# Block 3's x on one DMA queue, its scaling and its sums moved: a change to a linear attention and SwiGLU kernel

## The chip, the cores and the metric

The kernel runs on one core of a Trainium2 chip. A core has five engines, each with its own queue of instructions: TensorE (PE, matrix products; PEld is its loading of weights), VectorE (DVE), ScalarE (ACT), GpSimd (POOL) and SyncE (SP), which here only issues transfers. Transfers are issued from the queues of SP and ScalarE (in the profile SPq and ACTq) and carried out by 16 DMA engines. The metric is the time of one execution on the device in microseconds; less is better. The median of three runs before is 1026.51 us (1025.12 to 1028.15).

## The reference, cut to what matters

```python
def _attn_ref(q, k, v, g_norm):
    kv = np.einsum('bhsd,bhse->bhde', k, v)
    out = np.einsum('bhsd,bhde->bhse', q, kv)
    rms = np.sqrt(np.mean(out * out, axis=-1, keepdims=True) + 1e-06)
    return (out / rms * g_norm).astype(np.float32)

def _moe_ref(x, w_gate, w_val, w_out):
    g = x @ w_gate
    silu = g * (1.0 / (1.0 + np.exp(-g)))
    val = x @ w_val
    return (silu * val @ w_out).astype(np.float32)

# q, k, v: (8, 8, 576, 64), float32
x = np.ascontiguousarray(attn_out.transpose(0, 2, 1, 3)).reshape(4608, 512)
# w_gate, w_val: (512, 1536); w_out: (1536, 512)
return _moe_ref(x, w_gate, w_val, w_out)
```

A linear attention without a softmax, normalised and multiplied by a gain per channel, gives x; a SwiGLU feed-forward network with 1536 hidden channels follows.

## The kernel before, in words

The 4608 tokens are nine blocks of 512. Block 0 is computed with plain products. Blocks 1 and 2 are computed one at a time with a scheme of seven block products in place of eight (P1 to P7, on sums of sub-blocks of x and of the weights), and blocks 3 to 8 in pairs of blocks, with the scheme applied twice. Each block has an "up" part (gate, value, silu and their product, which gives h) and a "down" part (h times w_out). While one block is in its up part, the attention of a later block is computed in between.

The up part of a single block (class Up) runs over six pairs of hidden tiles. In `ahead`, pairs and steps are keyed as (pair, product), with pairs counted from 0; the sixth pair is 5. For each pair the products come in the order P1, P5, then P4 and P3 of the pair before, then P6, P2, P7; after the sixth pair follow its own P3 and P4 (`end`). Products go to banks of PSUM: b for P1, P6, P7, P4; a for P2; c for P5 and, accumulated onto it, P3. Each product has a follow-up on another engine:

- P1 and P6: ScalarE copies bank b (L677, L681).
- P2: VectorE adds bank a to a piece called s (L707, in the profile under the helper's line L130).
- P7: ScalarE copies bank b (L711) and applies silu to s (L714); VectorE adds bank c (L715, under L130). Behind it stand the "owed" sums of h of the pair before (L130 and L131, 128x256).
- P4: ScalarE applies silu (L724), POOL multiplies (L132).
- P3: VectorE adds bank c (under L130), POOL multiplies (L132).

During block 2's up part the x of block 3 is made. Its attention is normalised and turned by 32 x 32 squares on VectorE (L510); `place_x` then moves the squares to their places with 16 small DMAs within SBUF (L522), eight from SP's queue and eight from ScalarE's; `gain_x` multiplies by the gain, two activations on ScalarE (L529); `sum_steps` makes four sums of sub-blocks on VectorE (L539 to L542, under L130 and L131, arena<-arena 128x512). In the dictionary, `place_x` stands behind the fifth pair's P1, `gain_x` behind its P7, and the sums behind the sixth pair's P5. The sums go through a list of chores, of which at most two are taken after each product.

In block 2's up part VectorE's instructions keep the order in which the code makes them (`in_order`); on the other engines the framework's scheduler may move an instruction within what its data allow. In the built program the scaling of block 3's x stands on ScalarE between L711 and L714 of the sixth pair.

On SP's queue, around the placements, stand the loads of block 4's q (L333, 32 of them), then the placements, then 16 sends of weight pieces to DRAM (L920), then the loads of keys and values of block 5 (L312). Block 3's x lies in the first 14 units of a large SBUF tile, the arena, in the place of gate and value weights that have been sent away by then; the pieces sent at L920 lie from unit 16 up.

Of the kernel before, what the change touches and what calls it, by code (L numbers as in the profile page):

```python
# [18 lines left out]
def kernel(  # L19
# [41 lines left out]
    nc = tc.nc  # L61
# [65 lines left out]
    PAIRED = 3  # L127
# [102 lines left out]
    class Att:  # L230
# [284 lines left out]
        def place_x(self):  # L515
            src = self.turned.rearrange("p i (x c) -> p (i x) c", c=P)
            dst = self.x[:, 0:4].rearrange("p o k (t c) -> p (o k t) c", c=P)
            rows = [slice(32 * r, 32 * (r + 1)) for r in range(4)]
            for a in range(4):
                for b in range(4):  # L520
                    queue = nc.scalar if b % 2 else nc.sync
                    placed = queue.dma_start(out=dst[rows[b], :, rows[a]], in_=src[rows[a], :, rows[b]])  # L522
                    if b % 2 == 0:
                        self.placed = placed
# [421 lines left out]
    def raw_steps(j):  # L946


        for t, os in kept(j):
            yield lambda t=t, os=os: send_leaf(j, os, (1,), t[:, :, 0, 0])  # L950
            yield lambda t=t, os=os: send_leaf(j, os, (2, 3), t[:, :, 1].rearrange("p o e c -> p o (e c)"))

    def chunks(t):

        return t.rearrange("p f (s c) -> p (f s) c", c=P) if len(t.shape) == 3 else t.rearrange("p a b c -> p (a b) c")

    def kept_steps(j, room):


        for i, (t, os) in enumerate(kept(j)):  # L960
            b11, b12, b22 = t[:, :, 0, 0], t[:, :, 0, 1], t[:, :, 1, 1]
            to = room[:, 8 * i : 8 * (i + 1)].rearrange("p (o r) c -> p o r c", r=4)
            t2_ = to[:, :, 0]
            yield lambda b22=b22, b12=b12, t2_=t2_: sub(nc.vector, t2_, b22, b12)
            yield lambda b11=b11, t2_=t2_: add(nc.vector, t2_, t2_, b11)
            yield lambda t=t, t2_=t2_, to=to: sub(
                nc.vector, to[:, :, 2:4], t[:, :, 1], t2_.unsqueeze(2).to_broadcast([P, 2, 2, P])
            )
            yield lambda t2_=t2_, os=os: send_leaf(j, os, (6,), t2_)
            yield lambda b11=b11, t2_=t2_, to=to: sub(nc.vector, to[:, :, 1], b11, t2_)  # L970
            yield lambda to=to, os=os: send_leaf(
                j, os, (7, 4, 5), to[:, :, 1:4].rearrange("p o r c -> p o (r c)")
            )
        if j < 2:
            yield from raw_steps(j)
# [269 lines left out]
    def visit(ffn, att, gs, apart=False):  # L1245

        with tc.issue_after(ffn.multiplied.ins):
            for g in gs:
                att.kv(g, apart)
        if att.n < B:  # L1250
            ffn.visited = att.positions

    def ahead(ffn, att, then):

        def load(att, i):
            return lambda: ffn.sends.extend(att.quarter_steps(i, (0, 1), (nc.sync,)))

        def first():
            visit(ffn, att, (0, 1))
            ffn.sends += [load(att, 0), lambda: then.load_kv(0), load(att, 1)]  # L1260

        def turn(i):
            ffn.chores.append(lambda: att.turn_q(i))

        def second():
            visit(ffn, then, (0,), True)
            ffn.sends.append(lambda: then.load_kv(1))

        def half(i):
            with tc.issue_after(ffn.multiplied.ins):  # L1270
                att.heads(i, range(NS), (m_psum, m_psum))
            ffn.visited = att.multiplied
            ffn.chores += att.chores(i)
            if i:
                ffn.chores += att.turn_steps()

        def rest():
            for i in range(2):
                load(then, i)()

        def raw():
            for j in range(2, NP):
                ffn.sends += raw_steps(j)

        def sums():
            ffn.chores.extend(att.sum_steps())

        for j in (NP - 2, NP - 1):
            ffn.making.extend(kept_steps(j, chunks(h_alone[:, NF - 4 :]) if j == NP - 1 else chunks(xi_alone)))

        return {
            (0, 1): first, (1, 6): lambda: turn(0), (1, 7): second, (2, 1): lambda: half(0), (2, 6): lambda: turn(1),
            (2, 7): rest, (3, 1): lambda: half(1), (3, 7): lambda: visit(ffn, then, (1,), True), (4, 1): att.place_x,
            (4, 2): raw, (4, 7): att.gain_x, (5, 5): sums,
        }

    def alone(n):
# [27 lines left out]
        elif n == 1:  # L1325

            def third():
                visit(ffn, nxt, (0,))
                nxt.load_kv(1)

            def two_thirds():
                visit(ffn, nxt, (1,))
                for i in range(2):
                    nxt.load_q(i)

            ffn.up({(1, 7): third, (3, 7): two_thirds})
            nxt.turn()
            for g in range(2):
                blocks[PAIRED].load_kv(g)
        else:  # L1340
            with in_order(nc.vector.engine):
                ffn.up(ahead(ffn, nxt, blocks[PAIRED + 1]))
            nxt = blocks[PAIRED + 1]
            nxt.turn()
            for g in range(2):
                blocks[PAIRED + 2].load_kv(g)
# [82 lines left out]
```

## Time and profile before

| | us |
|---|---|
| median of three runs | 1026.51 |
| the profiled execution | 1027.35 |
| its span, first to last instruction | 1025.6 |
| PE busy | 998.6 |
| DVE busy | 667.0 |
| POOL busy | 368.6 |
| ACT busy | 232.1 |

Stages by time in the span, with the time in which PE was busy:

| stage | from, to | PE busy of |
|---|---|---|
| block 0 | 0 to 113.4 | 102.18 of 113.40 |
| block 0 down, block 1, its down | 113.4 to 265 | 149.60 of 151.60 |
| block 2 up | 265 to 363 | 89.85 of 98.00 |
| block 2 down | 363 to 401.5 | 38.50 of 38.50 |
| blocks 3 to 8 | 401.5 to 1025.6 | 618.51 of 624.10 |

The profile comes from one execution. A group of instructions is named by its line in the code, its engine, its operation and output<-input by the program's names; in the timeline a row gives start, duration, engine, line and how often, and in brackets the idle time of the engine just ahead with what ended it. That releaser is inferred; where an instruction waits for several things, it is the one that came last. SPq and ACTq rows are the issuing of transfers, not the transfers.

### The profile page before, as it was taken

Reading aid. Unit: us, or ns where it says so; the run is one execution under the profiler, and the core shown is the slowest. Engines: PE = TensorE matmul, PEld = TensorE weight load, DVE = VectorE, ACT = ScalarE, POOL = GpSimd, SP = SyncE. Lnnn points to the kernel's source line nnn. Section 1 sums busy time; section 2 is a strip of 40 time slices with the busy share of each in tenths; the row PEclk is TensorE's granted clock in tenths of the full one; section 3 lists DMA queues with packets and bytes.
Section 4 is the critical chain, followed back from the end, with each engine's and each line's share of the span. In section 5 each row is a group of like instructions: output and inputs, shape, how many; then the busy total and the mean of one; then the engine's idle time right before and its main releaser. Section 6 shows DMA issues by size and latency. Waiting matters only on the chain.

```text
span 1025.6 us, 17091 instructions
## 1 busy us (share of the span) xinstructions
PE 998.6 (97%) x6506; PEld 832.9 (81%) x6506; DVE 667.0 (65%) x1118; ACT 232.1 (23%) x367; POOL 368.6 (36%) x290
## 2 busy tenths in 40 slices
PE   5999999999999699999999999999999999999998
PEld 4544688888888588888888888888888888888887
DVE  2999797759766466566666846666767566666211
ACT  2765112221122211212111212112112121121100
POOL 0000273426343140454556003555650026546600
PEclk9999999999999899999999999999999999999999
DMA  8689643756663836676753265667321654553011
GB/s 233 201 255 263 119 90 118 226 161 148 179 163 63 214 67 156 168 212 166 169 139 58 89 149 160 156 173 182 101 32 52 144 156 144 153 145 97 1 42 42
DMA packets 254290, 143.23 MB, mean 140 GB/s; under 512 B 149504, under 2 KB 236544, under 8 KB 254208
## 3 DMA queue, kind: packets, MB, share of 16 engines
q1 hardware_dynamic: 219264, 137.67, 49.8%
q10 hardware_dynamic: 34880, 4.46, 2.7%
q8 instruction: 52, 0.85, 0.4%
q14 instruction: 30, 0.25, 0.1%
q0 software_dynamic: 64, 0.00, 0.0%
HBM read 104.99 MB, written 28.70 MB: 130 GB/s over the span
## 4 chain that ended last, share of the span: by engine, by line
PE 86%; DVE 5%; SPq 3%; DMA 2%; POOL 1%; ACT 1%; issue 1%; ACTq 0%; DVEq 0%; POOLq 0%
PE b L811 21%; PE b L661 21%; PE c L661 12%; PE c L811 11%; PE a L661 5%; PE a L811 5%; PE b L1154 4%; PE c L1154 4%; SPq L333 1%; DVE arena L131 1%; PE m L431 1%; PE m L370 1%; DMA arena<-in_v_dram 1%; POOL t L131 1%; DVE r L130 1%
## 5 line engine op out<-in xcount | busy, mean ns | idle before, releaser
L811 PE MATMUL b<-arena,t 128*128 128x256 f32 x1008 | 244.5, 381 | 0.0
L811 PEld LDWEIGHTS b<-arena,t 128*128 128x128 f32 x1008 | 190.0, 190 | 29.6 <-DVE r L130 2.5
L130 POOL TENSOR_TENSOR r<-r 128x256 f32<-128x256 f32 (+1 forms) x90 | 94.8, 1054 | 246.4 <-DMA t<-w 149.5
L130 DVE TENSOR_TENSOR r<-b,r 128x512 f32<-128x512 f32 (+1 forms) x234 | 138.9, 606 | 60.1 <-PE b L811 54.8
L130 DVE TENSOR_TENSOR r<-c,r 128x512 f32<-128x512 f32 (+1 forms) x170 | 104.6, 624 | 107.6 <-PE c L811 41.0
L132 POOL TENSOR_TENSOR arena<-r 128x1024 f32<-128x1024 f32 (+1 forms) x54 | 101.4, 1892 | 115.1 <-DVE r L130 89.0
L131 POOL TENSOR_TENSOR t<-wo 128x512 f32<-128x512 f32 x54 | 76.6, 1439 | 175.3 <-DVE wo L130 104.8
L130 DVE TENSOR_TENSOR r<-a,r 128x512 f32<-128x512 f32 x93 | 59.2, 636 | 108.6 <-PE a L661 71.0
L811 PE MATMUL c<-arena,t 128*128 128x256 f32 x504 | 122.5, 379 | 0.8 <-ACT r L825 0.8
L131 DVE TENSOR_TENSOR arena<-arena 128x512 f32<-128x512 f32 (+3 forms) x96 | 104.2, 1100 | 18.1 <-PE b L661 14.0
L811 PEld LDWEIGHTS c<-arena,t 128*128 128x128 f32 x504 | 95.6, 190 | 14.4 <-ACT r L825 1.2
L661 PE MATMUL b<-wo,arena 128*128 128x256 f32 x432 | 98.3, 382 | 0.6 <-issue 0.5
L661 PE MATMUL b<-t,arena 128*128 128x256 f32 x432 | 96.4, 379 | 1.4 <-POOL s L130 0.7
L661 PEld LDWEIGHTS b<-t,arena 128*128 128x128 f32 x432 | 81.9, 190 | 13.2 <-POOL s L130 1.1
L661 PEld LDWEIGHTS b<-wo,arena 128*128 128x128 f32 x432 | 81.2, 190 | 12.9 <-issue 0.9
L825 ACT COPY r<-b 128x512 f32<-128x512 f32 x54 | 31.6, 585 | 190.6 <-PE b L811 190.6
L131 POOL TENSOR_TENSOR t<-arena 128x512 f32<-128x512 f32 x36 | 51.1, 1432 | 59.5 <-PE c L661 20.2
L811 PE MATMUL a<-arena,t 128*128 128x256 f32 x252 | 66.1, 379 | 0.0
L811 PEld LDWEIGHTS a<-arena,t 128*128 128x128 f32 x252 | 47.9, 190 | 6.5
L661 PE MATMUL c<-wo,arena 128*128 128x256 f32 x216 | 48.2, 379 | 0.2 <-DVE r L130 0.2
L661 PE MATMUL c<-t,s 128*128 128x256 f32 x216 | 48.1, 379 | 0.0
L661 PE MATMUL a<-wo,arena 128*128 128x256 f32 x216 | 48.1, 379 | 0.0
(105 smaller groups left out, 1228.4 us busy)
## 6 DMA issues: line engine op xcount, KB each, us to landing
t<-w SPq DMA_DIRECT2D x180, 256.0 KB, 3.1
out_dram<-r SPq DMA_DIRECT2D x17, 512.0 KB, 2.9
ld<-in_k_dram SPq DMA_DIRECT2D x26, 288.0 KB, 4.6
ld<-in_v_dram SPq DMA_DIRECT2D x26, 288.0 KB, 5.8
t<-w SPq DMA_DIRECT2D x54, 128.0 KB, 2.2
ld<-in_moe_w_gate_dram SPq DMA_DIRECT2D x12, 512.0 KB, 4.7
ld<-in_moe_w_val_dram SPq DMA_DIRECT2D x12, 512.0 KB, 4.7
ld<-in_moe_w_out_dram SPq DMA_DIRECT2D x12, 512.0 KB, 4.9
```

Of the source, the lines that this page charges most:

```text
L130: add = lambda e, o, a, b: e.tensor_tensor(out=o, in0=a, in1=b, op=OP.add)
L131: sub = lambda e, o, a, b: e.tensor_tensor(out=o, in0=a, in1=b, op=OP.subtract)
L132: mul = lambda e, o, a, b: e.tensor_tensor(out=o, in0=a, in1=b, op=OP.mult)
L333: queue.dma_start(out=to[32 * r : 32 * (r + 1), j, g0:g1], in_=q[b, 4 * i + 2 * j + h, s0 : s0 + 32 * (g1 - g0), 32 * d : 32 * (d + 1)].re ...
L370: self.positions = nc.tensor.matmul(self.kv_ps[r][u * D : (u + 1) * D, g, :], lhsT=k[:, u, c, :], rhs=v[:, u, c, :], start=(c == 0), stop= ...
L431: self.multiplied = nc.tensor.matmul(self.ps[i][u][p : p + D, t, j, :], lhsT=self.qt[rows, tile_t, head, p : p + D], rhs=kvs[b % 3][rows, ...
L661: self.ffn.multiplied = nc.tensor.matmul(banks[e][:, e], lhsT=lhsT, rhs=rhs, start=first and i == 0 and (e == 0 or banks[0] is not banks[1 ...
L811: self.ffn.multiplied = nc.tensor.matmul(ps[:, i], lhsT=stream.use(self.ffn.n, self.j, o, p), rhs=self.operand(o, p), start=first and i == ...
L825: nc.scalar.copy(out=dst, in_=ps)
L1154: nc.tensor.matmul(t, lhsT=w[f // 2][:, i, P * (f % 2) : P * (f % 2 + 1)], rhs=x[:, i, of], start=(i == 0), stop=(i == NS - 1),)
```

## The change

In `place_x`, block 3 (`PAIRED` is 3) issues all 16 placements from SP's queue; for the other blocks half of them stay on ScalarE's. In `ahead`, the scaling moves from behind the fifth pair's P7 to behind the sixth pair's P5, and the sums from behind the sixth pair's P5 to behind its P6.

```diff
             for a in range(4):
                 for b in range(4):
-                    queue = nc.scalar if b % 2 else nc.sync
+                    queue = nc.scalar if b % 2 and self.n != PAIRED else nc.sync
                     placed = queue.dma_start(out=dst[rows[b], :, rows[a]], in_=src[rows[a], :, rows[b]])
                     if b % 2 == 0:
                         self.placed = placed
...
             (2, 7): rest, (3, 1): lambda: half(1), (3, 7): lambda: visit(ffn, then, (1,), True), (4, 1): att.place_x,
-            (4, 2): raw, (4, 7): att.gain_x, (5, 5): sums,
+            (4, 2): raw, (5, 5): att.gain_x, (5, 6): sums,
```

In the changed program's order of instructions, PE's and POOL's are the same as before. ScalarE has the scaling behind L714 of the sixth pair instead of ahead of it, and eight DMA issues fewer. SP has 16 placements in a row where it had eight. On VectorE the four sums stand behind the fifth pair's P3 addition and the sixth pair's P2 addition, the first two of them ahead of the sixth pair's P7 addition, the last two behind it and behind the owed sums of h.

## The prediction

> **What bounds the kernel now.** I read the page first, then PE's waits, the table of stages around the only place where its clock share drops, the timeline there, and SP's waits. The page:
>
> ```profile
> span 1025.6 us, 17091 instructions
> PE 998.6 (97%) x6506; PEld 832.9 (81%) x6506; DVE 667.0 (65%) x1118; ACT 232.1 (23%) x367; POOL 368.6 (36%) x290
> PEclk9999999999999899999999999999999999999999
> ```
>
> TensorE is the bound: 27 us of the span are not PE. One slice, the 14th, has a lower clock, and it lies where the change works. The longest wait in PE's list:
>
> ```profile
> PE c L661 <- DVE r L130: 8.9, 3, 8.2
> ```
>
> One wait of 8.2 us on an addition of VectorE. The stages around it (PE, PEld, DVE, ACT, POOL busy, granted clock, DMA share, GB/s):
>
> ```profile
> 348.00:356.60 8.60, 0.46 (x3) 0.06 (x1) 5.37 (x8) 3.28 (x4) 1.64 (x1) 0.75 1.01 274
> 356.60:360.00 3.40, 3.39 (x8) 2.77 (x9) 0.71 (x2) 0.02 (x1) 0.00 (x0) 0.50 1.06 228
> 360.00:363.00 3.00, 3.00 (x9) 2.42 (x9) 0.69 (x1) 0.00 (x0) 1.26 (x1) 0.58 0.96 203
> 363.00:366.00 3.00, 3.00 (x16) 2.64 (x15) 0.72 (x2) 0.60 (x1) 1.26 (x1) 1.00 0.01 1
> ```
>
> PE stands still from 348.46 to 356.61 and then runs at half clock until about 362.5. The timeline of the hole, instruction by instruction:
>
> ```profile
> 346.57 1.89 PE L661 MATMUL b<-arena,t 128*128 128x256 f32 x8
> 348.50 0.58 ACT L711 COPY r<-b 128x512 f32<-128x512 f32 x1 [2.87 <-PE b L661]
> 348.98 2.19 ACT L529 ACTIVATE arena<-arena,gain 128x1024 f32<-128x1024 f32 x2
> 351.20 0.69 DVE L130 TENSOR_TENSOR arena<-arena 128x512 f32<-128x512 f32 x1 [10.37 <-DMA w<-arena]
> 351.81 0.68 DVE L131 TENSOR_TENSOR arena<-arena 128x512 f32<-128x512 f32 x1
> 352.41 0.68 DVE L130 TENSOR_TENSOR r<-c,r 128x512 f32<-128x512 f32 x1
> 353.01 2.35 DVE L131 TENSOR_TENSOR arena<-arena 128x512 f32<-128x512 f32 x2
> 355.28 0.68 DVE L130 TENSOR_TENSOR r<-a,r 128x512 f32<-128x512 f32 x1
> 355.88 0.68 DVE L130 TENSOR_TENSOR r<-c,r 128x512 f32<-128x512 f32 x1
> 355.99 0.63 ACT L714 ACTIVATE r<-r 128x512 f32<-128x512 f32 x1 [4.83 <-DVE r L130]
> 356.61 3.78 PE L661 MATMUL c<-arena 128*128 128x256 f32 x8 [8.15 <-DVE r L130]
> ```
>
> This is read backwards. PE's P3 of the sixth pair accumulates onto bank c, which the sixth pair's P7 addition (L715, the row at 355.88) must have read; it ends at 356.56 and PE starts 0.05 later. Ahead of it in VectorE's queue stand the first sum of block 3's x (351.20) and five others. That sum had held VectorE for 10.37 us. The view names a DMA w<-arena as its releaser; I don't believe it: the sum reads x, which the scaling L529 writes, and the second scaling ended at 348.98 + 2.19 = 351.17, 0.03 before it; the weight pieces sent at L920 lie in the arena from unit 16 up, block 3's x in units 0 to 14. The scaling in turn waited for nothing but its place in ScalarE's queue, behind L711 (348.50): the last of its placing DMAs was issued at 341.04. On the issuing side, the waits of SP's queue and then the timeline:
>
> ```profile
> SPq L333 <- DMA arena<-r: 11.3, 1, 11.3
> ```
>
> ```profile
> 326.94 5.83 ACTq L522 DMA_DIRECT2D arena<-r  x6
> 335.67 5.37 SPq L522 DMA_DIRECT2D arena<-r  x8
> 341.08 9.55 SPq L920 DMA_DIRECT2D w<-arena  x16
> ```
>
> SP's loads of q (L333) waited 11.3 us for a placing DMA that ScalarE had yet to issue, because in the built program the DMAs of the two queues take their completion counters in turn from the same eight, and a DMA waits for the last one on its counter; SP's own eight placements therefore start only at 335.67.
>
> **What the Trainium skill says.** "TensorE: Matmul & The Clock Gate", section "What's actually happening": the array falls to half clock after an idle window of about 3.4 us and recovers after a busy one, the windows running freely. The trace agrees: clock share 0.75, 0.50, 0.58, 1.00 in the four rows above. The same page, "Architectural detail", says that ScalarE and VectorE are strict first-in-first-out; the ten microseconds in which VectorE has a ready addition of bank c behind a waiting sum show it. "DMA: Bandwidth & Descriptors", "Issuing engines are not separate DMA queues": both issuers' DMAs run on the same 16 DMA engines, and a second issuer saves only its time to initiate. Here initiating costs 5.37/8 = 0.67 us each on SP, so eight more cost 5.4 us of SP. "ScalarE: Activation LUTs", "What ACT_TABLE_LOAD costs", prices a switch of sets at 2.66 us, which a silu directly ahead of a scaling might bring; the trace has two such loads in all (1283 ns each, the last at 31.4), with copies, scalings and silus mixed ever since, so I take none.
>
> **The change, part by part.** *Placement on SP alone.* ScalarE loses eight issues. They delayed the fifth pair's P4 silu (L724) to 332.81, 3.3 us after its product, but PE ran through, so this is worth 0. SP gains eight issues and loses the 11.3 us wait: 15 loads of q are left at 316.2 (the first of the 16 in SP's row from 315.80 to 335.50 is issued then), about 0.5 each as on their unhindered stretches, done near 324; placement can start when the transposes end (322.48 + 2.36 = 324.84). Sixteen at 0.67 + 0.04 last 11, to 336, and land 2.3 to 4.3 later (all L522 DMAs): by 340. Were the old start of 335.67 kept, the last would be issued by 346.6 and landed by 349 to 351. Queued behind on SP: 16 weight pieces (9.6 us) and the key and value loads of block 5. In before they started at 341.08 and 350.73; now about 336 and 346 (at worst 346.6 and 356). SP next waits 21.5 us for PE, so both ends of this cost 0.
>
> *Sums one product on.* On VectorE the changed program's order is: fifth pair's P3 addition, sixth pair's P2 addition, two sums, sixth pair's P7 addition, the fifth pair's two h sums, then the other two sums. So the P3 addition runs at 343.3 (PE's product of 341.39 + 1.89) and the P2 addition at 344.84 + 1.89 = 346.73, done by 347.5: both leave the hole. Of the sums two instead of four stand ahead of the P7 addition.
>
> *Scaling behind P5.* On ScalarE the scalings now stand behind the sixth pair's silu L714 instead of ahead of it. That silu waited for the P2 addition (355.99 before); that is now done at 347.5, so it starts right behind L711 at 348.98. From there (starts of successive ScalarE instructions lie about 0.10 less than a duration apart):
>
> silu 348.98 to scaling 349.51 (0.63 - 0.10); scalings end 349.51 + 2.19 = 351.70; first sum 351.73, second 352.34, P7 addition 352.94, ended 353.62; PE at 353.67.
>
> Before, PE started at 356.61: **2.94 us less**. Cross-check: out of VectorE's stretch go the P3 addition (352.41 to 353.01), two sums (353.01 to 355.28) and the P2 addition (355.28 to 355.88), 3.47 in all; the silu ahead of the scaling gives 0.53 back. If the silu cost a table load, 2.66 would return; if nothing, 0; I take 0.
>
> *Clock.* The hole shrinks from 8.15 to 5.21 us. Half clock lasted from 356.61 to about 362.5, worth half of 5.9, 2.95 us. Is 5.2 us idle enough to drop the clock again? Windows fall anywhere; in the worst position the hole is split into 2.6 and 2.6. At the program's end the clock record falls to half at 1024.7 with the last matmul ended at 1022.2, a window with 2.5 idle: so a split hole drops it too. I take the loss as unchanged: in both kernels half clock then lasts one to two windows, 3.4 to 6.8 us by the page's figure, an estimate of 1.7 to 3.4 lost. Bounds of what a shorter hole can bring: 0 and 2.95.
>
> *Behind it.* From 363 to 401.5 PE is busy for all of 38.5 us, and from there 618.5 of 624.1; what precedes (h sums, POOL's products) hangs on PE's P3 and P4 and moves with them. A shift at 356 should reach the end whole.
>
> Sum: -2.94. The profiled execution took 1027.35 around its span of 1025.6, 0.84 above the median of 1026.51; so 1024.4 for it and **1023.6** for the median.
>
> **Rivals.** *The clock stays up:* the hole is too short. For it: 5.2 is not two windows. Against: the fall at the end after 2.5 idle. Time: 1026.51 - 2.94 - 2.95 = 1020.6. *Given back:* a transfer ordered by SP or POOL ends a later stage, so the shift is absorbed. For it: the DMA share is 1.0 in the hole. Against: PE's wait list shows no DMA after the start. Time: 1026.5. *Slower, placement late on one queue:* if SP's q loads still end at 335.67 and an issue takes 1.2 (the slowest L522 issue) rather than 0.67, the sixteenth ends at 354.9, lands at 359.2 with 4.3, and the scaling starts 9.7 later than I say: PE at 363.4, time 1026.5 + 6.8 = 1033.3. It decides once the last landing passes 349.5, and the kernel is slower once it passes 352.45. Against: the load ahead of it no longer waits for ScalarE.
>
> **How the numbers follow.** No change means within 0.3%, 3.1 us, about what can be told here; my forecast lies just inside it, so its own spread splits it. Forecast 0.84 (own range 1022 to 1025.3; 0.40 beyond 0.3%, 0.43 within, 0.01 slower), clock stays up 0.08 (faster), given back 0.05 (same), placement late 0.03 (slower). Faster 0.48, same 0.48, slower 0.04. The three times shown spread over 3 us, partly where the clock's windows fall. Range 1020.3 to 1025.8: it takes in the clock rival and leaves out the other two.
>
> **What would show it.** Right: PE's wait before P3 near 5.2 us; silu L714 near 349, scalings near 349.5; placement on SP from about 325; SP's 11.3 us wait gone; half clock still there behind the hole. Wrong: the scaling waiting for arena<-r, a table load beside L714, full clock at once after the hole, or a new PE wait between 363 and 401.

## The result, and the profile after

The changed kernel takes 1024.78 us (median of ten runs, 1023.59 to 1026.13), the kernel before beside it 1026.89: ratio 0.998, with a 95% interval of 0.997 to 0.999. A second set of runs, made with the later experiments, gave 1024.35 against 1026.87 (ratio 0.9975, 0.9965 to 0.9985). So 2.1 to 2.5 us are gained, where 2.94 were forecast; the two intervals, 1.0 to 3.1 us and 1.5 to 3.6 us in time, both take in the forecast.

The same views as before, now of the changed kernel. The page:

```profile
span 1024.4 us, 17093 instructions
PE 998.7 (97%) x6506; PEld 832.7 (81%) x6506; DVE 667.3 (65%) x1118; ACT 232.1 (23%) x367; POOL 369.8 (36%) x290
PEclk9999999999999899999999999999999999999999
```

PE's work is the same, and the 14th slice still has the lower clock. Its list of waits (in total, times, longest):

```profile
PE c L661 <- DVE r L130: 5.9, 3, 5.2
```

Where one wait lasted 8.2 us, the longest is now 5.2. The hole is the idle time of PE ahead of the sixth pair's P3. Its timeline (start, duration, engine, line; in brackets the idle time ahead and what ended it):

```profile
328.55 10.75 SPq L522 DMA_DIRECT2D arena<-r  x16
339.34 9.32 SPq L920 DMA_DIRECT2D w<-arena  x16
...
348.33 1.89 PE L661 MATMUL b<-arena,t 128*128 128x256 f32 x8
348.60 0.69 DVE L130 TENSOR_TENSOR r<-a,r 128x512 f32<-128x512 f32 x1 [2.83 <-PE a L661]
...
350.74 0.63 ACT L714 ACTIVATE r<-r 128x512 f32<-128x512 f32 x1
351.27 2.17 ACT L529 ACTIVATE arena<-arena,gain 128x1024 f32<-128x1024 f32 x2
...
353.48 0.69 DVE L130 TENSOR_TENSOR arena<-arena 128x512 f32<-128x512 f32 x1 [4.18 <-ACT arena L529]
354.09 0.68 DVE L131 TENSOR_TENSOR arena<-arena 128x512 f32<-128x512 f32 x1
354.69 0.68 DVE L130 TENSOR_TENSOR r<-c,r 128x512 f32<-128x512 f32 x1
...
355.43 3.78 PE L661 MATMUL c<-arena 128*128 128x256 f32 x8 [5.21 <-DVE r L130]
```

Everything here stands 1.76 us later than in the profile before (P7 at 348.33, not 346.57), because of longer waits at the start of the program and around 121 us, far ahead of the change. Subtract it and the chain is the forecast one: silu L714 directly behind L711, scaling behind the silu, two sums, the P7 addition, PE. The hole is 5.21 us, and the first sum's wait has fallen from 10.37 to 4.18. The sixth pair's P2 addition (348.60) runs right behind its product. The 16 placements start at 328.55, right behind the last load of q, and are issued by 339.30; the trace has the last of them landed at 340.73, 10.5 us ahead of the scaling.

The stages behind the hole (busy of PE, PEld, DVE, ACT, POOL, then granted clock, DMA share, GB/s):

```profile
348.00:354.00 6.00, 2.22 (x11) 1.61 (x9) 1.22 (x2) 3.19 (x4) 0.00 (x0) 0.95 1.02 276
354.00:360.00 6.00, 4.57 (x11) 3.63 (x12) 4.12 (x8) 0.00 (x0) 0.00 (x0) 0.50 1.05 235
360.00:363.00 3.00, 3.00 (x15) 2.62 (x14) 0.00 (x0) 0.60 (x1) 2.06 (x2) 0.96 0.17 36
```

Half clock is there again, from 353.4 to 360.2. PE is busy at half clock from 355.43, so for 4.8 us, which loses 2.4; before it was 5.9 us and 2.95.

### The profile page after: what moved, and what is told of

It reads as the page before. It is cut to its first block, busy times and chain, and to the rows that moved or that the text cites. A ratio compares the mean times of both kernels' runs of the same rounds, so it can differ in the third digit from the quotient of the medians.

```text
span 1024.4 us, 17093 instructions
## 1 busy us (share of the span) xinstructions
PE 998.7 (97%) x6506; PEld 832.7 (81%) x6506; DVE 667.3 (65%) x1118; ACT 232.1 (23%) x367; POOL 369.8 (36%) x290
## 4 chain that ended last, share of the span: by engine, by line
PE 76%; DVE 9%; DMA 5%; SPq 5%; issue 2%; ACT 2%; POOL 1%; DVEq 0%; POOLq 0%; ACTq 0%
PE b L811 21%; PE b L661 21%; PE c L661 11%; PE c L811 10%; PE a L661 5%; PE a L811 5%; SPq L333 2%; DVE r L190 1%; PE m L431 1%; DMA ld<-in_moe_w_out_dram 1%; DVE arena L131 1%; PE m L370 1%; DVE arena L199 1%; SPq L522 1%; DMA ld<-in_v_dram 1%
```

## The experiments

The profiles can be compared without the program's start by one measure: from the start of the sixth pair's P7 (the PE row `b<-arena,t` ahead of the hole) to the end of the span. It is 1025.55 - 346.57 = 678.98 us before and 1024.36 - 348.33 = 676.03 after, so in these two profiles the change is worth 2.95 us, hole and clock together. From the start of P3 to the end it is 668.94 and 668.93, so the difference is all in the hole: half clock took 0.55 us less from PE behind it, and about as much was lost again further on. The table has the measure from P7 for all experiments.

| kernel | hole before P3 | P7 at | P7 to end | time, median (runs) |
|---|---|---|---|---|
| before | 8.15 | 346.57 | 678.98 | 1026.89 (10) |
| changed | 5.21 | 348.33 | 676.03 | 1024.78 (10) |
| changed, second set (e6) | 5.21 | 346.37 | 675.43 | 1024.35 (8) |
| queue edit alone (e1) | 8.15 | 346.92 | 678.25 | 1026.94 (13) |
| moves alone (e2) | 5.21 | 351.11 | 675.06 | 1024.34 (21) |
| silu behind scaling (e5) | 4.69 | 346.88 | 674.75 | 1023.4 (1) |
| sums another product on (e9) | 1.40, and 3.27 later | 346.49 | 675.32 | 1023.21 (9) |
| scaling and sums early (e4; e10) | 1.40 | 346.64; 345.87 | 669.15; 669.53 | 1017.62 (4); 1017.27 (4) |
| the same, old queues (e7) | 1.40 | 346.56 | 669.41 | 1017.6 (4) |
| placements three times (e8) | 16.74 | 347.84 | 686.71 | 1036.32 (1) |
| changed, hole filled (e3; e12) | filled | 346.59; 346.50 | 673.36; 674.36 | 1021.76 (6); 1021.69 (6) |
| before, hole filled (e11) | filled | 346.66 | 677.30 | 1026.08 (13) |

**e1, the queue edit alone.**

```diff
-                    queue = nc.scalar if b % 2 else nc.sync
+                    queue = nc.scalar if b % 2 and self.n != PAIRED else nc.sync
```

> Only the queue edit: all 16 placements on SP, scaling and sums where they were. Theory (the hole is made by the order on ScalarE and VectorE, not by when the placements land): SP's placements start near 325 to 329 and the 11.3 us wait of SP is gone, but the scaling still stands behind L711 and the hole before P3 stays at 8.15 us; time as before, within 0.5 us. Rival (the earlier placement is what pays): hole below 6 us, 2 us or more faster than before.

The ratio to the kernel before is 1.0002 (0.9994 to 1.001). Its timeline:

```profile
325.33 11.38 SPq L522 DMA_DIRECT2D arena<-r  x16
...
349.33 2.19 ACT L529 ACTIVATE arena<-arena,gain 128x1024 f32<-128x1024 f32 x2
351.55 0.69 DVE L130 TENSOR_TENSOR arena<-arena 128x512 f32<-128x512 f32 x1 [10.27 <-ACT arena L529]
...
356.34 0.63 ACT L714 ACTIVATE r<-r 128x512 f32<-128x512 f32 x1 [4.83 <-DVE r L130]
356.96 3.78 PE L661 MATMUL c<-arena 128*128 128x256 f32 x8 [8.15 <-DVE r L130]
```

SP's wait of 11.3 us is gone from its list, the placements start 10 us sooner, and nothing follows: the hole is 8.15 us to the hundredth. The reason is that even on two queues they were in time: in the profile before, the last one landed at 342.92, 6 us ahead of the scaling at 348.98.

The row at 351.55 bears on the releaser too. The stall is the one that the profile before put down to a DMA w<-arena; here the view names the scaling. A name in the view alone doesn't settle it, since in e2 it is w<-arena again, but the times do: in all 14 profiles, with the scaling early or late, the first sum starts 0.03 us after the scaling's end. Where another event ends within some hundredths of a microsecond, the view can name the wrong one.

**e2, the moves alone.**

```diff
-            (4, 2): raw, (4, 7): att.gain_x, (5, 5): sums,
+            (4, 2): raw, (5, 5): att.gain_x, (5, 6): sums,
```

> Only the move of scaling and sums; placements half on ScalarE as before. Theory: the whole effect is here, hole 5.2 us, 2 to 3 us faster than before, although SP still waits 11 us and places from about 335. Rival (the moved sums need the earlier placement): hole over 6.5 us, less than 1.5 us faster.

1024.34 us, ratio 0.9978 (0.9971 to 0.9985): the whole effect. From SP's list of waits and the timeline:

```profile
SPq L333 <- DMA arena<-r: 8.4, 1, 8.4
```

```profile
339.50 5.37 SPq L522 DMA_DIRECT2D arena<-r  x8
...
354.05 2.17 ACT L529 ACTIVATE arena<-arena,gain 128x1024 f32<-128x1024 f32 x2
...
356.25 0.69 DVE L130 TENSOR_TENSOR arena<-arena 128x512 f32<-128x512 f32 x1 [4.18 <-DMA w<-arena]
...
358.20 3.78 PE L661 MATMUL c<-arena 128*128 128x256 f32 x8 [5.21 <-DVE r L130]
```

SP still waits for ScalarE's placements and places late, and the hole is 5.21 all the same. One thing more shows in the order of the built program: with the sums alone moved, and the scaling left behind the fifth pair's P7 in the dictionary, every engine's order is the same as in this kernel, so on top of the sums' move the line that moves the scaling changes nothing. The sums' move lets the P2 addition go ahead of them on VectorE; that makes the silu L714 ready sooner, which is probably why the scheduler puts it ahead of the scaling. (This is the order of the two built programs; no run has the sums' move alone.)

**e3, the changed kernel with the hole filled.**

```diff
         def end(self):
+            if self.ffn.n == 2:
+                ps = m_psum.tile([P, 2, HB], F32, name="m")
+                for _ in range(12):
+                    nc.tensor.matmul(ps[:, 0], lhsT=ident, rhs=wo[:, 0, 0:HB], start=True, stop=True)
```

> The changed kernel with 12 matrix products more (128 rows, 256 columns, result unused) on PE ahead of the sixth pair's P3, 5.2 us of work laid into the 5.2 us hole. Theory (the idle hole drops the clock, and that costs 1.7 to 3.4 us in the changed kernel too): no half clock near 355, P3 takes 1.9 us instead of 3.78, time 1.7 to 3.4 us below the changed kernel, about 1022.3. Rival (the half clock comes from something else in that stretch, such as the full DMA queues): P3 still at 3.78, time as the changed kernel or up to 0.5 us more.

PE's timeline:

```profile
348.32 5.34 PE L738 MATMUL m<-wo,ident 128*128 128x256 f32 x24
353.69 1.99 PE L661 MATMUL c<-arena 128*128 128x256 f32 x8
355.52 1.89 PE L661 MATMUL b<-arena,t 128*128 128x256 f32 x8
```

The useful work starts no sooner, but eight matmuls of P3 take 1.99 us, not 3.78, and the time is 1021.76, 3.0 below the changed kernel. The idle hole itself drops the clock, not the DMA traffic, which is as dense here (share 1.04 from 348 to 354, against 1.02 in the changed kernel). So what the half clock costs the changed kernel is the size forecast for it (1.7 to 3.4): 3.0 between the medians, and 2.7 and 2.1 from P7 to the end against its two profiles.

**e4 and e10, scaling and sums early.** The scaling is issued behind the fifth pair's P7 again, and the sixth pair's P6 copy is held behind it in ScalarE's order, so that the scheduler can't put it back; the sums are made at once and not through the chores.

```diff
+                self.gained = nc.scalar.activation(out=x, in_=x, func=ACT.Copy, scale=gain)
...
+            gained = blocks[PAIRED].gained if self.ffn.n == 2 and getattr(self, "j", 0) == NP - 1 else None
+            with tc.issue_after(gained.ins) if gained else ExitStack():
+                nc.scalar.copy(out=self.u2, in_=self.ps["b"])
...
-            (4, 2): raw, (5, 5): att.gain_x, (5, 6): sums,
+            (4, 2): raw, (4, 7): att.gain_x, (5, 6): att.sums,
```

> The changed kernel with the scaling held ahead of the sixth pair's P6 copy on ScalarE, and all four sums on VectorE between the fifth pair's P3 addition and the sixth pair's P2 addition. Theory (the placements have landed by 342 and the hole is only queue order): scaling from about 344 to 346.1, sums done by 348.6, hole near 1.3 us (a copy of 0.58 and an addition of 0.68), clock up; 2.94 + 3.9 + 2.5 below before, about 1017.6. Rival (the scaling would then wait for placements or delay the P6 copy and so PE): PE waits before P7 or P6, hole over 3 us, time above 1021.

> The early version (scaling ahead of the sixth pair's P6 copy, sums behind P6) once more. Theory: wait before P3 1.4 us, mean granted clock 1.0, the median between 1017.2 and 1018.0. What is open is its spread: the first set of runs lay within 0.2 us, the same with the old queues within 2.1. If the spread of the kernel before came from its half clock alone, these runs lie within 0.5; if part of it comes from the start of the program, they spread over 1 to 2 us.

The timeline of the first of the two:

```profile
342.16 2.18 ACT L529 ACTIVATE arena<-arena,gain 128x1024 f32<-128x1024 f32 x2
344.37 1.61 DVE L130 TENSOR_TENSOR arena<-arena 128x512 f32<-128x512 f32 x1 [0.28 <-ACT arena L529]
345.90 2.13 DVE L131 TENSOR_TENSOR arena<-arena 128x512 f32<-128x512 f32 x3
347.95 0.68 DVE L130 TENSOR_TENSOR r<-a,r 128x512 f32<-128x512 f32 x1
...
349.19 0.69 DVE L130 TENSOR_TENSOR r<-c,r 128x512 f32<-128x512 f32 x1 [0.55 <-ACT r L711]
...
349.93 1.99 PE L661 MATMUL c<-arena 128*128 128x256 f32 x8 [1.40 <-DVE r L130]
```

All of block 3's x is scaled and summed before the P7 product ends; the P7 addition now waits only for the copy L711, and 1.40 us of hole remain. The clock stays up: its mean share is 0.999 or 1.0 in every run of e4, e10 and e7. The times are 1017.62 (ratio 0.9912, 0.9899 to 0.9925) and 1017.27 (0.9913, 0.9898 to 0.9928): about 9 us below the kernel before and 7 below the changed one. This is the version to take. The spread that e10 asked about: 0.2 us in the first set, 1.0 in the second and 2.1 in e7, with four runs in each. So something other than the half clock contributes, as e10's second case said. P7 starts at 345.87 to 346.64 in the three profiles, so a part of it can come from the start of the program; how much isn't shown.

**e5, the silu behind the scaling.** The changed kernel, with L714 of the sixth pair held behind the scaling (an added line makes it L715).

```diff
-                nc.scalar.activation(out=x, in_=x, func=ACT.Copy, scale=gain)
+                self.gained = nc.scalar.activation(out=x, in_=x, func=ACT.Copy, scale=gain)
...
-            with tc.issue_after(copied.ins):
+            gained = blocks[PAIRED].gained if self.ffn.n == 2 and self.j == NP - 1 else copied
+            with tc.issue_after(copied.ins), tc.issue_after(gained.ins):
                 nc.scalar.activation(out=self.s, in_=self.s, func=ACT.Silu)
```

> The changed kernel with the sixth pair's silu L714 held behind the two scalings. Theory (the hole is the chain scaling, two sums, P7 addition, PE): the scaling starts right behind L711, 0.53 us earlier, and PE's wait before P3 is 5.21 - 0.53 = 4.7 us; the silu, now 2.2 us later, is waited for by nobody on the path; half clock still there, one time 0.5 us below the changed kernel's, within its spread. Rival (the silu is needed early, by POOL's product or a later addition): the wait before P3 is not shorter than 5.2, or a new wait of PE stands between 356 and 366.

```profile
349.28 2.19 ACT L529 ACTIVATE arena<-arena,gain 128x1024 f32<-128x1024 f32 x2
351.37 0.62 ACT L715 ACTIVATE r<-r 128x512 f32<-128x512 f32 x1
...
353.45 3.78 PE L661 MATMUL c<-arena 128*128 128x256 f32 x8 [4.69 <-DVE r L130]
```

The hole is 0.52 shorter, against 0.53 forecast, and no other wait appears behind it. So the silu's 0.53 from start to start is the price of the order that the scheduler chose, and having the silu beside a scaling brings no other cost. The single time, 1023.4, is within the changed kernel's runs and can't show half a microsecond.

**e6, the changed kernel once more.** No edit.

> The changed kernel once more, for its distance from the kernel before. Theory: the wait before P3 is 5.2 us against 8.15, worth 2.94, and the half clock behind it costs as much or a little more than in the kernel before, so the median lies 2.0 to 2.9 us below it, 1024.0 to 1024.9. Rival (the shorter hole sometimes leaves the clock up): runs near 1021.5 and a mean granted clock of 1.0 in some of them.

The time is inside the range of the theory, and no run is near 1021.5. In all 18 runs of the changed kernel the mean granted clock is below 1 (0.996 to 0.998), so 5.2 us of hole always dropped it. In the 77 runs of the kernel before that stood beside the experiments it is 0.9958 in the mean, in the changed kernel's 18 it is 0.9967. Twice the missing share of the time gives the time at half clock: about 8.6 us (2 x 0.0042 x 1025) and 6.8 (2 x 0.0033 x 1023). These figures take in what there is of half clock at the program's end, under a PE that has finished.

The half clock became shorter by 1.8 us and the hole by 2.94. Only half clock under a busy PE costs anything, and how much of it that is depends on when in the hole the clock falls: 3.8 and 2.7 us after PE stopped in the two profiles with the longer hole (before, e1), 3.2, 2.5 and 2.4 in three with the shorter (changed, e6, e2). If that delay is the same on average, half clock under a busy PE became 2.94 - 1.8 = 1.1 us longer, an estimate of half a microsecond more lost, about what the medians lack. The profiles say the opposite (2.95 and 2.38 lost with the longer hole; 2.40, 2.08 and 1.99 with the shorter), but those two aren't typical. Their share is below 0.995, with 10.24 us at half clock, and in 34 of the 77 runs of the kernel before it is 0.997, which leaves 7.2 us at most; the median of those 34 is 1026.25, that of the other 43 is 1027.43. So on average the loss may have become larger or smaller by half a microsecond, and the runs don't say which.

**e7, early with the old queues.** The early version with the first hunk undone.

> The early version (scaling ahead of the sixth pair's P6 copy) with the placements on both queues as before. They are then issued until about 341 in place of 336 and landed by 343.4 to 345.3. Theory (the queue edit is worth next to nothing): the scaling waits for them up to some 1 to 2 us longer than at 342.2, the P7 addition has 0.55 us of that to spare, PE's wait before P3 is 1.4 to 2.3 us, 1017.6 to 1018.5. Rival (with an early scaling the queue edit carries the gain): the scaling starts after 346, the wait is over 3 us and the clock drops: over 1020.5.

```profile
340.69 9.54 SPq L920 DMA_DIRECT2D w<-arena  x16
...
342.63 2.19 ACT L529 ACTIVATE arena<-arena,gain 128x1024 f32<-128x1024 f32 x2 [0.46 <-DMA w<-arena]
...
349.85 1.99 PE L661 MATMUL c<-arena 128*128 128x256 f32 x8 [1.40 <-DVE r L130]
```

Placements that are issued until 340.65 put the scaling off by 0.5 us: the last one lands at 342.53 in the trace, 0.1 ahead of the scaling, though the view names w<-arena here too. The P7 addition has that to spare, so the hole is 1.40 and the time that of the early version. The queue edit is worth nothing here either.

**e8, the placements three times over.**

```diff
-            for a in range(4):
+            for a in [*range(4)] * (3 if self.n == PAIRED else 1):
```

> The changed kernel with the 16 placements issued three times over, 48 on SP's queue, for how much later they may land before it costs. Theory: 48 x 0.67 = 32 us from about 325 (328.5 where q's last load is late as in the changed kernel's profile), so the last is issued at 357 to 361 and landed by 360 to 364; the scaling waits for it (releaser arena<-r) and PE's wait before P3 grows from 5.2 to 15 us or more; 1034 to 1040. Rival (the scaling waits for something else than the placements, or the last copy is not waited for): the wait stays at 5.2 and the time within 1 us of the changed kernel's.

```profile
328.44 32.33 SPq L522 DMA_DIRECT2D arena<-r  x48
...
362.30 2.19 ACT L529 ACTIVATE arena<-arena,gain 128x1024 f32<-128x1024 f32 x2 [11.42 <-DMA arena<-r]
...
366.47 3.40 PE L661 MATMUL c<-arena 128*128 128x256 f32 x8 [16.74 <-DVE r L130]
```

Now the scaling's releaser is arena<-r: it starts at 362.30, 0.1 us after the last placement landed (362.19 in the trace). In the changed kernel the last one landed 10.5 us before the scaling, and that is the slack behind which one queue for all 16 costs nothing. Here it is used up, and what is beyond it reaches the hole in full: the scaling's start moves from 351.27 - 348.33 = 2.94 behind P7's start to 362.30 - 347.84 = 14.46, 11.5 more, and the hole grows by 16.74 - 5.21 = 11.5.

**e9, the sums one product further on.**

```diff
-            (4, 2): raw, (5, 5): att.gain_x, (5, 6): sums,
+            (4, 2): raw, (5, 5): att.gain_x, (5, 7): att.sums,
```

> The changed kernel with the sums one more product on, behind the sixth pair's P7 in place of its P6. In the built program the scaling then stands behind the sixth pair's P4 silu (L724) and all four sums behind the P7 addition and the owed sums of h. Theory (the hole is only the queue order around the P7 addition): the P7 addition runs right behind L711, PE's wait before P3 is 1.4 us as in the early version and the clock stays up; the scaling starts near 354, the four sums end near 359 and hold up the sixth pair's P3 addition and its sums of h to about 362, against 361 for the second product of the down part, which may wait up to 2 us for them: 1017.6 to 1019.6. Rival (given back in the down part): the late sums of h stop PE for 4 us or more behind 358 and the clock drops there, 1021 or more.

```profile
349.78 1.99 PE L661 MATMUL c<-arena 128*128 128x256 f32 x8 [1.40 <-DVE r L130]
...
354.03 2.18 ACT L529 ACTIVATE arena<-arena,gain 128x1024 f32<-128x1024 f32 x2
...
356.24 0.69 DVE L130 TENSOR_TENSOR arena<-arena 128x512 f32<-128x512 f32 x1 [5.66 <-ACT arena L529]
356.85 2.13 DVE L131 TENSOR_TENSOR arena<-arena 128x512 f32<-128x512 f32 x3
358.90 0.68 DVE L130 TENSOR_TENSOR r<-c,r 128x512 f32<-128x512 f32 x1
...
359.66 1.37 POOL L132 TENSOR_TENSOR arena<-r 128x512 f32<-128x512 f32 x1 [4.17 <-DVE r L130]
...
361.09 2.08 PE L661 MATMUL b<-wo,arena 128*128 128x256 f32 x4 [3.27 <-POOL arena L132]
```

The stages there (columns as before; the last three are granted clock, DMA share and GB/s):

```profile
357.00:360.00 3.00, 0.82 (x4) 0.38 (x2) 2.85 (x5) 0.00 (x0) 0.34 (x1) 1.00 0.60 136
360.00:363.00 3.00, 1.91 (x4) 1.18 (x4) 0.43 (x1) 0.00 (x0) 2.40 (x3) 0.52 0.00 0
```

The first half of the theory held: hole 1.40, P3 at full clock. The second didn't. The same wait moved one place down: VectorE stands at the first sum for 5.66 us with the sixth pair's P3 addition (358.90) behind it, and POOL's product behind that. I had this due at the second product of the down part, near 361; the last four of the first product's 24 matmuls need it already, at 357.8. PE waits 3.27 us, and the clock falls to half from about 360 in this profile and below 1 in seven of nine runs. 1023.21, ratio 0.9965 (0.9954 to 0.9976): better than the change by about 1 us, and 6 behind the early version. That is the rival's outcome, though its 4 us were too many.

**e11 and e12, both kernels with the hole filled.** e12 is e3 again; e11 is the same edit to the kernel before, with `range(18)` for its longer hole.

> The kernel before with 18 products whose result nobody reads (128x256, into a bank of the other attention's, left out of the output) ahead of the sixth pair's P3, so that PE is busy through the 8.15 us. It takes the half clock out of the comparison. Theory (the 2.94 us of the shorter hole reach the end whole, and the missing 0.5 to 0.8 us is in the half clock or in the runs' spread): clock 1.0, P3 at full clock (1.99 us for eight), the time 2.9 us above the changed kernel with such products, which runs beside it. Rival (part of the shift is given back later, whatever the clock does): 2.0 to 2.4 us above it.

> The changed kernel with 12 such products ahead of the sixth pair's P3, once more, as the other half of the comparison with the kernel before so treated. Theory: clock 1.0, 1021.4 to 1022.1, 2.9 us below that kernel. Rival (shift given back in part): the two are 2.0 to 2.4 us apart.

```profile
348.39 7.93 PE L738 MATMUL m<-wo,ident 128*128 128x256 f32 x36
356.71 1.99 PE L661 MATMUL c<-arena 128*128 128x256 f32 x8 [0.39 <-DVE r L130]
```

From P7 to P3 it is 10.05 us here and 353.60 - 346.50 = 7.10 in e12: 2.95 apart. The medians are 1026.08 and 1021.69, 4.4 apart, which neither theory had. From P7 to the end the two profiles differ by 677.30 - 674.36 = 2.94, as the theory had it. But both have about 1 us more behind P3 (667.25 and 667.26) than the other profiles that stay at full clock (665.87 to 666.27 in e3, e4, e7 and e10). In e11 it is a wait of 1.1 us near 462 for which the profile shows no releaser (`PE m L370 <- issue`), and e12's six runs spread over 5 us. So the experiment speaks against the rival, a smaller difference, but it measures no size, and e11's 0.9 below the kernel before isn't the price of its half clock.

## Why the prediction was right, point by point

**Queue order makes the hole.** Right. VectorE's first sum, the scaling behind L711 and the P7 addition behind the sums hold in every profile: delay the scaling by 11.5 and the hole grows by 11.5 (e8), take 0.53 from ahead of it and it shrinks by 0.52 (e5), take it all away and 1.40 is left (e4). The doubted releaser was indeed wrong (e1, and the 0.03 us in every profile).

**Placement on SP alone at 0.** Right, by e1 and e7. The cover was named as SP's early start, and the landing measures it: 10.5 us in the changed kernel, used up in e8. With the old queues it was 6 us already, so there was nothing to gain. The start itself was read 2 us too early in this profile (324.84 plus its 1.76 of shift is 326.6, found 328.55), because the last load of q came between; in e1 it was 325.33, as forecast.

**Sums one product on, scaling behind the silu: 2.94 less.** Right to the hundredth: 8.15 - 5.21, in three profiles of the order (changed, e6, e2), and each step of its chain lies where it was forecast once the 1.76 us are taken off. No table load came. What the prediction told less well is which line does it: it lists the two moves as two steps, and the built order is that of the sums' move alone.

**Clock: loss unchanged.** Right in that half clock is still there: that the clock would stay up, the first rival, occurred in none of 18 runs. The size is less sure. In the single profiles the loss under busy PE went from 2.95 to 2.4, filling the hole brought 2.7 to 3.0 in the medians, and the average before and after is open by half a microsecond (e6). The 2.95 that was read before is that of a profile with the longer half clock, which 34 of 77 runs don't have.

The page "TensorE: Matmul & The Clock Gate", "What's actually happening", on whose free-running windows of about 3.4 us this rested, agrees with these records in the lengths: the half clock lasts 10.24 us before and 6.83 in the changed kernel, three and two times 3.41, where the prediction took one to two. In the condition it doesn't fit: the page has the clock fall after an idle window, but in e5 PE was busy for 1.3 of the 3.41 us ahead of the fall. The prediction's own argument, that a window idle in part is enough, is what these runs bear out.

**The shift reaches the end whole.** Right as far as single profiles tell: from P7 to the end 2.95 us less in the first profile and 3.55 in the second (678.98 - 675.43), and no new wait of PE from 356 to 402 in either. That the first agrees with 2.94 to the hundredth is luck, since in it 0.55 us of shorter half clock were lost again behind it. Of "given back", which forecast no gain at all, nothing is left; a part given back of half a microsecond can't be told from the spread.

**The sum.** The medians fell by 2.1 and 2.5 (and by 2.5 in e2), 0.4 to 0.8 less than forecast. Each interval takes in 2.94, e2's barely (1.5 to 3.0), but all three lie below it. Two terms can be off: the clock's loss, taken as unchanged (e6), and the last step, that a shift in the profile is the shift of the medians. P7 starts between 345.87 and 351.11 in these profiles, though what runs before it differs little, and a median of ten runs carries some of that. In the profile that came with the result P7 stood 1.76 later than before, so its span shows 1.2 less and not 2.95. Which of the two it is isn't settled.

## What to carry to other kernels

Where an engine stands for microseconds before an instruction of low urgency, look behind it in the same queue for the one that the bound engine waits for: the cure is the order, and moving the work a product later helps only if what is then behind it isn't due either (here the late sums held up a product of POOL's and stopped PE again; the early ones held up nothing). Before crediting a transfer that has been sped up, find the slack between its landing and its reader: there were 6 us of it before the edit, so the edit was worth nothing. Look at more than the name of a releaser where two events end together. And compare two profiles from the last instruction ahead of the change to the end, since the start moves by microseconds from run to run.

## What the runs showed of the hardware that was not expected

Short holes are enough for half clock. One of 3.27 us in the profile went with it in seven of nine runs (e9), one of 5.21 in 18 of 18. With 1.40 us the clock share stayed at 0.999 or 1.0 in all 12 runs of the early version, and a single step of 3.41 us at half clock would make it 0.998. PE needn't be idle for 3.41 us on end ahead of the fall: it came 2.1 us after PE stopped in e5, and 2.3 after in e9.

In these profiles half clock comes in steps of 3.41 us: 6.83 us after holes of 3.27, 4.69 and 5.21, 10.24 after 8.15, 17.07 after 16.74. A step in which PE is busy for only a part doesn't end it: in the kernel before PE was busy for 2.5 of the 3.41 us up to 359.10, and the next step was at half clock again. The length isn't fixed by the hole alone: after 8.15 us, 34 of 77 runs have at most 7.2 us by their clock share.

In e2's profiled run half clock set in a second time, at 126.66 for one such step, behind two waits of 0.8 and 0.9 us in block 1's attention, with PE busy for half of the 3.41 us just before; P7 came at 351.11 there, and the run took 1027.93, the highest of its 21. So a pair of waits that is usually harmless can now and then cost some microseconds, which may be part of the spread of all these kernels.
